# Two cached-attention decodes in one kernel: 4 MB loads of 32 KB descriptors, a softmax per four heads, and one TensorE loop

## The chip, the cores and the metric

The kernel runs on one core of a Trainium2 chip. The metric is the device time of one execution in microseconds (us). Four runs of the kernel before gave 249.22 to 249.61 us, with a median of 249.45 us. One further execution was profiled; its own time is 249.4 us, and all durations below come from it.

## The reference

Two independent attention decodes, A and B, of one token each. The model width is 576; there are 32 query heads, 16 key/value heads, a head size of 128, and a cache of 8192 positions. A looks only at the last 2048 positions, B at all 8192. The two results of 576 numbers stand side by side in the output. All tensors are bfloat16.

```python
def _A_ref(x, k_cache, v_cache, wq, wo):
    W = min(4096, max(256, Sk // 4))                       # 2048
    q = (x @ wq).reshape(B, Sq, Hq, Dh).transpose(0, 2, 1, 3)
    k = jnp.repeat(k_cache[:, :, Sk - W:, :], rep, axis=1)
    v = jnp.repeat(v_cache[:, :, Sk - W:, :], rep, axis=1)
    p = _softmax(jnp.einsum("bhqd,bhkd->bhqk", q, k) * (Dh ** -0.5), axis=-1)
    o = jnp.einsum("bhqk,bhkd->bhqd", p, v)
    return o.transpose(0, 2, 1, 3).reshape(B, Sq, Hq * Dh) @ wo
```

B is the same without the cut to W. Each input byte is used once: 8.4 MB each for A's K and V, 33.6 MB each for B's K and V, and 4.7 MB for each of the four weight matrices, 102.8 MB in all.

## The kernel before

**A planner.** The kernel is a list of operations, each with an engine, what it reads and what it writes (`Program.add`, L55). The planner derives semaphore waits from the list (`wants`, L104). Each engine runs its operations in the order in which they were added. SP issues all large loads, ACT issues the two loads of x. TensorE's (PE's) operations in the middle are folded into hardware loops (`looped`, L214 onwards): an outer loop over V rounds holds an inner loop over K rounds, and the waits of a loop body must be the same in every pass. All engines start after a barrier that the framework puts first (L743).

**Buffers.** `kslots` and `vslots` hold four slots each of 128 partitions x 16 KB (2 MB). `kt` holds four transposed units of 8 KB a partition. A load into a slot has to wait until the slot's last reader is done, and SP issues its loads strictly in order, so a load that waits holds back all that follow.

**Start.** wq of A goes into `vslots` 0 and 1 and a part of `kslots` 3, wq of B into `vslots` 2 and 3 and another part of `kslots` 3, each in loads of 2 MB, 2 MB and 0.5 MB (`load_wq`). x arrives as 128 rows of five bfloat16 numbers (`load_x`, L344); DVE masks it into `xpad` (L410), and PE multiplies it with wq (`q_part`, L425). `q_finish` turns the result into columns.

**K rounds.** There are five: round 0 is A's K, rounds 1 to 4 are B's. A round loads four slots. Each slot is two units; PE transposes a unit in 32 matmuls (L466), ACT and DVE evict them to `kt` (L472, L475), and PE multiplies the unit with the queries in 8 matmuls (L486) that add to the scores in `sacc`. B's round holds eight heads at 4096 positions, and two rounds share one `sacc`, one softmax and one run of 16 transposes of the weights (`softmax_exp`, `softmax_transpose` L536, `put` L545). `scores_zero` (L497) clears `sacc`. So there are three softmaxes.

**V rounds.** Five, each of four slots. Per slot PE runs 64 matmuls (`v_slot`, L557). DVE picks the diagonal blocks (`v_keep`, L566, and the sum of L373). The order on PE is K rounds 0 and 1, V 0, K 2 and 3, V 1, K 4, V 2, V 3, V 4.

**End.** Before V round 4 the last outer pass runs `weights` for A and B (L581 to L613: maximum, exponentials and sums over the parts, a chain of small steps through PE, DVE and ACT), and spreads A's output into `opj` (L630, L634). wo comes in nine loads: 14, 14 and 4 rows of A into `kslots` 0 to 2, 14 rows of B into `kslots` 3, and 8, 4, 3, 2 and 1 rows of B into `vslots` 0 and 1 (a row is 576 numbers a partition, 147,456 bytes over 128 partitions). All nine follow V round 4 on SP's queue. `wo_part` (L646) uses four matmuls a row; `finish_out` copies and stores.

Of the kernel before, what the change touches and what calls it, by code (L numbers as in the profile page):

```python
# [20 lines left out]
TS = 64  # L21
WQ_UNITS = 9
WQ_U = 2048
OUTW = DM // 4
# [14 lines left out]
class Program:  # L39
# [15 lines left out]
    def add(self, eng, fn, reads=(), writes=(), dma=None, after=(), tag=None, inc=1, loop=None):  # L55
        op = Op(eng, fn, tuple(reads), tuple(writes), dma, tag, 16 if dma is not None else inc, loop)
# [77 lines left out]
    def waits_of_loop(self, ops):  # L134
# [9 lines left out]
        for key, places in points.items():  # L144
# [26 lines left out]
            if len(fixed) == len(places):  # L171
                for place, hi in fixed.items():
# [4 lines left out]
                   for n in (1, 2, 16) for first in (0, n) if fits(first, n, some, taker)]  # L177
# [9 lines left out]
    def emit(self):  # L187
# [15 lines left out]
        def looped(eng, ops):  # L203
# [15 lines left out]
            def parts(of, i):  # L219
                todo = sorted(p for p in body if body[p].loop[3] == of)  # L220
                while todo:
                    cond = body[todo[0]].loop[2]
                    n = next((k for k, p in enumerate(todo) if body[p].loop[2] is not cond), len(todo))
                    if cond is None:
                        some(todo[:n])
                    else:
                        with eng.If(cond(i)):
                            some(todo[:n])
                    todo = todo[n:]

            with eng.Fori(0, self.outer) as v:
                with eng.Fori(*self.rounds_of(v)) as g:
                    parts("inner", g)
                parts("outer", v)

        def run(name, eng):
            ops = per[name]
            inside = [k for k, o in enumerate(ops) if o.loop]
            if not inside:
                plain(eng, ops)  # L240
                return
            lo, hi = inside[0], inside[-1] + 1
            assert len(inside) == hi - lo
            plain(eng, ops[:lo])
            looped(eng, ops[lo:hi])
            plain(eng, ops[hi:])

# [22 lines left out]
def bass_concat_heads__sliding_block_cached__gqa_block_cached__decode_kernel(  # L270
# [20 lines left out]


    G = [4, 2]
    CHUNK = [0, 1, 1, 2, 2]
    KIND = [0, 1, 2, 1, 2]
    base = [SK - W_A, 0]

    prog = Program(nc)
    add = prog.add
# [3 lines left out]
    kt = nc.alloc_sbuf_tensor("kt", [128, NKT, UNIT], BF16)  # L303
# [4 lines left out]
    pick = nc.alloc_sbuf_tensor("pick", [128, 4, 128], F32)  # L308
    same = nc.alloc_sbuf_tensor("same", [128, 128], F32)
    selq = nc.alloc_sbuf_tensor("selq", [128, 4], BF16)  # L310
    onesf = nc.alloc_sbuf_tensor("onesf", [128, 4], F32)
    zero = nc.alloc_sbuf_tensor("zero", [128, 512], BF16)
    qtm = nc.alloc_sbuf_tensor("qtm", [128, 3 * 256], BF16)
    qst = nc.alloc_sbuf_tensor("qst", [128, NS * 64], BF16)
    xtwo = nc.alloc_sbuf_tensor("xtwo", [128, 2, 8], BF16)
# [6 lines left out]
    srow = nc.alloc_sbuf_tensor("srow", [1, 2, 256], F32)  # L322
    diag = nc.alloc_sbuf_tensor("diag", [128, 2, DH, NS], F32)
    acc = nc.alloc_sbuf_tensor("acc", [128, 7, DH], F32)
# [11 lines left out]
    B_M = ("bank", 7)  # L336


    def load_x(P):
        def go(act):  # L340
            x = xs[P]
            with nc.allow_non_contiguous_dma(reason="small x load"):
                src = bass.AP(tensor=x.tensor, offset=x.offset, ap=[[9, 64], [4, 2], [1, 5]])
                return act.dma_start(xtwo[:, P, 0:5], src)  # L344
        add("act", go, writes=[("xtwo", P)], dma="x%d" % P)
# [5 lines left out]
    def setup(pool):  # L351
        for t in (ident, xpad, selq, zero, warm, qtm, identf, same, pick):
# [4 lines left out]
    add("pool", setup, writes=["ident", ("xpad", 0), ("xpad", 1), "selq", "ones", "warm", "zero", "identf", "pick", "same",  # L357
                               ("qtm", 0), ("qtm", 1), ("qtm", 2), ("opj", 0), ("opj", 1)])
# [13 lines left out]
    def sums(out, view, reads, writes, tag=None):  # L372
        add("dve", lambda dve: dve.tensor_reduce(out, view, AX.X, ALU.add), reads=reads, writes=writes, tag=tag)  # L373
# [5 lines left out]
    def load(dst, src, writes, dma, after=()):  # L379
        add("sp", lambda sp: sp.dma_start(dst, src()), writes=writes, dma=dma, after=after)  # L380

    def load_wq(P, k, dst, n, res):
        lo = 4 * k * WQ_U
        load(dst, lambda: wqs[P].rearrange("(m r) n -> m (r n)", m=64)
             .rearrange("m (e y) -> (m e) y", e=2)[:, lo:lo + n * WQ_U], [res], "wq%d%d" % (P, k))

    def load_kv(arrs, g, s, slots, name, after=()):
        P = 0 if g == 0 else 1
        i = s if g == 0 else 4 * ((g - 1) % 2) + s
        ch = 128 // G[P] * TS  # L390
        r0 = base[P] + (0 if g == 0 else (g - 1) // 2 * ch)

        def src():
            return arrs[P][0, i * G[P]:(i + 1) * G[P], r0:r0 + ch, :].rearrange("g (p t) d -> p g (t d)", t=TS)
        load(slots[:, s, :], src, [(name, s)], "%s%d" % (name, s), after)


    K_ON = lambda g: g < 5
    ODD = lambda g: (g & 1) == 1
    V_OF = {1: 0, 3: 1, 4: 2, 5: 3, 6: 4}  # L400

    def rounds_of(v):
        return v + 2 - (v < 2) - (v < 1), v + 3 - (v < 1)

    prog.rounds_of, prog.outer = rounds_of, len(V_OF)


    def x_columns(P):
        for e in range(2):
            add("dve", lambda dve, e=e: dve.tensor_scalar(xpad[:, P, 5 * e:5 * e + 5, 0], xtwo[:, P, 0:5],  # L410
                                                          par2[:, e:e + 1], None, ALU.mult),
                reads=[("xtwo", P), "par2"], writes=[("xpad", P)])
# [4 lines left out]
    def q_part(P, k, n, src, res):  # L417
        def mm(pe):
            for u in range(4 * k, 4 * k + n):
                for c in range(2):  # L420
                    for j in range(4):
                        n_ = 2 * j + c
                        x = u // 2 if n_ // 4 == u % 2 else 5 + (u + 1) // 2
                        o = (u - 4 * k) * WQ_U + (n_ % 4) * 512
# [3 lines left out]
        add("pe", mm, reads=[("xpad", P), res], writes=qbank)  # L428

    def q_finish(P):  # L430
# [13 lines left out]
        def put(dve):  # L444
            for e in range(2):
                if P == 0:
                    dst = bass.AP(tensor=qtm, offset=e, ap=[[768, 128], [4, 2], [34, 2], [72, 4]])
                else:
                    dst = bass.AP(tensor=qtm, offset=256 + e, ap=[[768, 128], [68, 2], [34, 2], [136, 4]])
                src = opsum[:, 0:32].rearrange("p (b a e j) -> p b a e j", b=2, a=2, e=2)[:, :, :, e, :]  # L450
                ins = dve.tensor_copy(dst, src)
            return ins
        add("dve", put, reads=[B_O], writes=[("qtm", 0)] if P == 0 else [("qtm", 1), ("qtm", 2)])

    def q_stage(g, s):
        o = KIND[g] * 256 + s * 64
        add("pool", lambda pool: pool.tensor_copy(qst[:, s * 64:(s + 1) * 64], qtm[:, o:o + 64]),  # L457
            reads=[("qtm", KIND[g])], writes=[("qst", s)], tag="q%d" % s)

    def k_transpose(g, u, place):  # L460
        s, half = divmod(u, 2)
        for q in range(4):
# [6 lines left out]
            add("pe", tr, reads=[("k", s), "ident"], writes=[("bank", q)], loop=(g, place + q / 8, K_ON, "inner"))  # L469
            dst = kt[:, u % NKT, q * 1024:(q + 1) * 1024]  # L470
# [8 lines left out]
    def k_scores(g, u, place):  # L479
        s, half = divmod(u, 2)  # L480

        def mm(pe):
            for e in range(2):
                for j in range(4):
                    rhs = kt[:, u % NKT, j * 1024:(j + 1) * 1024].rearrange("d (x g) -> d x g", g=2)[:, :, e]
                    ins = pe.matmul(sacc[32 * j:32 * j + 32, 512 * half:512 * half + 512],  # L486
                                    lhsT=qst[:, s * 64 + e * 32:s * 64 + e * 32 + 32],
                                    rhs=rhs, start=False, stop=True, skip_group_check=True)
            return ins
        add("pe", mm, reads=[("qst", s)] + [("kt", u % NKT, q) for q in range(4)], writes=[B_S[half]],  # L490
            loop=(g, place, K_ON, "inner"))

    def scores_zero(loop):
        for h in range(2):
            def mm(pe, h=h):
                for j in range(4):
                    ins = pe.matmul(sacc[32 * j:32 * j + 32, 512 * h:512 * h + 512], lhsT=zero[:, 0:32], rhs=zero[:, :],  # L497
                                    start=True, stop=True, skip_group_check=True)
                return ins
            add("pe", mm, reads=["zero"], writes=[B_S[h]], loop=loop and (loop[0], loop[1] + h / 8) + loop[2:])  # L500


    C_M, C_NB, C_L, C_W, C_AL, C_T = 0, 2, 4, 6, 8, 10
# [4 lines left out]
    def softmax_exp(c):  # L508
        P, k = (0, 0) if c == 0 else (1, c - 1)
# [18 lines left out]
    def softmax_transpose(g, place):  # L528
        for u in range(2):
# [9 lines left out]
            add("pe", tr, reads=["psb", "ident"], writes=[bank], loop=(g, place + u / 8, ODD, "inner"))  # L539
# [7 lines left out]
            add("dve", put, reads=[bank, "par2"], writes=[("ptm", u)], tag="put%d" % u, inc=1 if g == 1 else 2)  # L547


    def v_slot(vg, s, place, g):  # L550
# [10 lines left out]
        add("pe", mm, reads=[("ptm", 0), ("ptm", 1), ("v", s)], writes=[B_O], loop=(g, place, None, "outer"))  # L561

    def v_keep(g):
        def go(dve):
            m = bass.AP(tensor=rows, offset=KIND[g] * NS, ap=[[3 * NS, 128], [0, DH], [1, NS]])
            return dve.tensor_tensor(diag[:, g % 2, :, :], opsum[:, :].rearrange("p (s d) -> p d s", s=NS), m, ALU.mult)  # L566
        add("dve", go, reads=[B_O, "rows"], writes=[("diag", g % 2)])
        sums(acc[:, g, :], diag[:, g % 2, :, :], [("diag", g % 2), B_O], [("acc", g)], tag="ext")


    LAST = lambda v: v == 4

    def weights(P):
        n = 1 + P
        at = [(6, 18 + P + k / 8, LAST, "outer") for k in range(3)]
        m = C_M
        if n > 1:
            add("dve", lambda dve: dve.tensor_reduce(st(P, C_T), st(P, C_M, n), AX.X, ALU.max),
                reads=[("st", P, C_M + c) for c in range(n)], writes=[("st", P, C_T)])
            m = C_T  # L580
        add("pe", lambda pe: pe.matmul(misc[0:1, 0:128], lhsT=st(P, m), rhs=identf[:, :], start=True, stop=True),  # L581
            reads=[("st", P, m), "identf"], writes=[B_M], loop=at[0])
# [175 lines left out]
```

## Time and profile before

| what | value |
|---|---|
| median of four runs | 249.45 us |
| profiled execution, its own time | 249.4 us |
| its span, from the first to the last instruction | 248.0 us |
| PE busy | 169.9 us (69%) |
| ACT, DVE, POOL busy | 87.0, 81.0, 12.9 us |
| bytes read from HBM | 102.76 MB |
| SP waited for PE transposes (L466), in total | 85.0 us in 15 waits |
| SP waited for PE's V matmuls (L557), in total | 74.7 us in 14 waits |

The span is 1.4 us shorter than the execution's own time; that remainder lies outside the instructions. Busy time of an engine says how long its instructions ran, not whether anything waited for them. The 16 DMA engines of the core work beside the compute engines, and the page gives their busy share and the bytes they moved in 40 slices of 6.2 us. SP's waits are for buffers that are still in use; a wait delays the stream of bytes only where the DMA engines have nothing else left to move.

### The profile page before, as it was taken

Reading aid. Unit: us, or ns where it says so; the run is one execution under the profiler, and the core shown is the slowest. Engines: PE = TensorE matmul, PEld = TensorE weight load, DVE = VectorE, ACT = ScalarE, POOL = GpSimd, SP = SyncE. Lnnn points to the kernel's source line nnn. Section 1 sums busy time; section 2 is a strip of 40 time slices with the busy share of each in tenths; the row PEclk is TensorE's granted clock in tenths of the full one; section 3 lists DMA queues with packets and bytes.
Section 4 is the critical chain, followed back from the end, with each engine's and each line's share of the span. In section 5 each row is a group of like instructions: output and inputs, shape, how many; then the busy total and the mean of one; then the engine's idle time right before and its main releaser. Section 6 shows DMA issues by size and latency. Waiting matters only on the chain. (4 is left out here: it accounts for less than half of the span.)

```text
span 248.0 us, 7504 instructions
## 1 busy us (share of the span) xinstructions
PE 169.9 (69%) x3406; PEld 130.9 (53%) x3406; DVE 81.0 (33%) x152; ACT 87.0 (35%) x92; POOL 12.9 (5%) x49
## 2 busy tenths in 40 slices
PE   0174789984999569995999637998256144594634
PEld 0031267763777458864878427785244133484522
DVE  0010064663555026554555122656005004204000
ACT  2000066837378018876578004875300000000000
POOL 7500000000000000000000000000000000000000
PEclk9997599997799979999899965999858755557555
DMA  6999999999999999999999999999999999999993
GB/s 256 405 414 422 441 436 418 426 426 431 428 427 428 426 423 423 430 431 426 431 431 423 428 428 431 428 433 426 428 426 426 431 428 431 431 429 421 420 410 149
DMA packets 8236, 102.92 MB, mean 415 GB/s; under 512 B 1185, under 2 KB 1313, under 8 KB 2081
## 3 DMA queue, kind: packets, MB, share of 16 engines
q1 hardware_dynamic: 7936, 102.77, 98.0%
q8 instruction: 8, 0.13, 0.2%
q10 hardware_dynamic: 288, 0.00, 0.1%
q14 instruction: 4, 0.02, 0.0%
HBM read 102.76 MB, written 0.00 MB: 414 GB/s over the span
## 5 line engine op out<-in xcount | busy, mean ns | idle before, releaser
L472 ACT ACTIVATE kt<-ktps 128x1024 bf16<-128x1024 bf16 x80 | 77.7, 1021 | 52.1 <-PE ktps L466 52.1
L466 PEld LDWEIGHTS ktps<-ident,kslots 128*128 128x128 bf16 x1280 | 77.5, 102 | 26.1 <-issue 26.0
L466 PE MATMUL ktps<-ident,kslots 128*128 128x128 bf16 x1280 | 83.8, 228 | 10.5 <-PEq L214 10.4
L475 DVE COPY kt<-ktps 128x1024 bf16<-128x1024 bf16 x80 | 55.2, 691 | 51.3 <-PE ktps L466 51.3
L557 PE MATMUL opsum<-vslots,ptm 128*32 128x128 bf16 x1280 | 27.8, 260 | 28.4 <-PEq L214 24.4
L557 PEld LDWEIGHTS opsum<-vslots,ptm 128*32 128x32 bf16 x1280 | 24.9, 118 | 32.1 <-issue 32.0
L486 PE MATMUL sacc<-kt,qst 128*32 128x512 bf16 x320 | 25.9, 392 | 1.9 <-PEq L214 1.8
L566 DVE TENSOR_TENSOR diag<-opsum,rows 128x512 f32<-128x512 f32 x5 | 3.5, 692 | 56.0 <-PE opsum L557 56.0
L425 PE MATMUL opsum<-vslots,xpad 128*32 128x512 bf16 x64 | 8.6, 521 | 16.9 <-DVE xpad L410 11.3
L599 ACT ACTIVATE stat<-stat 128x1 f32<-128x1 f32 (+1 forms) x2 | 0.6, 294 | 37.3 <-DVE stat L597 37.3
L425 PEld LDWEIGHTS opsum<-vslots,xpad 128*32 128x32 bf16 x64 | 2.3, 122 | 20.3 <-issue 13.0
L457 POOL COPY qst<-qtm 128x64 bf16<-128x64 bf16 x20 | 4.5, 236 | 123.3 <-PE sacc L486 115.2
L431 ACT ACTIVATE qrow<-opsum 128x512 bf16<-128x512 f32 x2 | 1.2, 597 | 26.2 <-PE misc L425 26.2
L646 PE MATMUL ktps<-kslots,opj 128*32 128x144 bf16 x184 | 6.1, 326 | 5.8 <-DMA kslots<-in_B_wo_dram 3.9
L486 PEld LDWEIGHTS sacc<-kt,qst 128*32 128x32 bf16 x320 | 5.4, 95 | 8.8 <-issue 5.1
L523 ACT ACTIVATE psb<-sacc,stat 128x2048 bf16<-128x2048 f32 x3 | 5.9, 1967 | 8.5 <-DVE stat L517 8.5
L425 PE MATMUL misc<-vslots,xpad 128*32 128x512 bf16 x64 | 8.7, 523 | 0.0
L646 PEld LDWEIGHTS ktps<-kslots,opj 128*32 128x32 bf16 x184 | 5.2, 145 | 6.4 <-DMA kslots<-in_B_wo_dram 4.2
L433 DVE CAST qrow<-misc 128x512 bf16<-128x512 f32 x2 | 1.4, 692 | 17.8 <-PE misc L425 17.8
L630 PE MATMUL misc<-acc,pick 128*128 128x32 f32 x16 | 3.8, 404 | 3.6 <-DVE acc L624 2.9
L652 DVE CAST outsb<-ktps 128x144 bf16<-128x144 f32 x2 | 0.6, 308 | 16.1 <-PE ktps L646 16.1
L630 PEld LDWEIGHTS misc<-acc,pick 128*128 128x128 f32 x16 | 3.6, 328 | 3.8 <-DVE acc L624 3.0
(66 smaller groups left out, 63.0 us busy)
## 6 DMA issues: line engine op xcount, KB each, us to landing
kslots<-in_B_k_cache_dram SPq DMA_DIRECT2D x16, 2048.0 KB, 20.5
vslots<-in_B_v_cache_dram SPq DMA_DIRECT2D x16, 2048.0 KB, 18.8
kslots<-in_A_k_cache_dram SPq DMA_DIRECT2D x4, 2048.0 KB, 30.4
vslots<-in_A_v_cache_dram SPq DMA_DIRECT2D x4, 2048.0 KB, 25.1
vslots<-in_A_wq_dram SPq DMA_DIRECT2D x2, 2048.0 KB, 10.0
vslots<-in_B_wq_dram SPq DMA_DIRECT2D x2, 2048.0 KB, 20.5
kslots<-in_A_wo_dram SPq DMA_DIRECT2D x2, 2016.0 KB, 23.8
kslots<-in_B_wo_dram SPq DMA_DIRECT2D x1, 2016.0 KB, 31.2
```

What stands on the lines that cost most here:

```text
L425: ins = pe.matmul(qps[c][32 * j:32 * j + 32, :], lhsT=xpad[:, P, x, :], rhs=src[:, o:o + 512], start=(u == 0), stop=(u == WQ_UNITS - 1))
L433: add("dve", lambda dve: dve.tensor_copy(qrow[:, 512:1024], misc[:, :]), reads=[B_M], writes=[("qrow", 1)])
L457: add("pool", lambda pool: pool.tensor_copy(qst[:, s * 64:(s + 1) * 64], qtm[:, o:o + 64]), reads=[("qtm", KIND[g])], writes=[("qst", s)], ...
L466: ins = pe.matmul(ktps_bf[q][:, t * 128:(t + 1) * 128], lhsT=kslots[:, s, o:o + 128], rhs=ident[:, :], start=True, stop=True, is_transpose ...
L472: add("act", lambda act, q=q, dst=dst: act.activation(dst, ktps_bf[q], ACT.Copy), reads=[("bank", q)], writes=[("kt", u % NKT, q)], tag="e ...
L475: add("dve", lambda dve, q=q, dst=dst: dve.tensor_copy(dst, ktps_bf[q]), reads=[("bank", q)], writes=[("kt", u % NKT, q)], tag="e%d%d" % ( ...
L486: ins = pe.matmul(sacc[32 * j:32 * j + 32, 512 * half:512 * half + 512], lhsT=qst[:, s * 64 + e * 32:s * 64 + e * 32 + 32], rhs=rhs, start ...
L523: return act.activation(psb[:, :].rearrange("p (x g) -> p x g", g=2), src, ACT.Exp, bias=st(P, C_NB + k), scale=SCALE, accum_out=st(P, C_L ...
L557: ins = pe.matmul(opsum[32 * j:32 * j + 32, s * DH:(s + 1) * DH], lhsT=ptm[:, o:o + 32], rhs=vslots[:, s, b * 128:(b + 1) * 128], start=(u ...
L566: return dve.tensor_tensor(diag[:, g % 2, :, :], opsum[:, :].rearrange("p (s d) -> p d s", s=NS), m, ALU.mult)
L630: ins = pe.matmul(misc[:, 0:32], lhsT=pick[:, r, :], rhs=acc[:, d, 32 * r:32 * r + 32], start=(r == 0), stop=(r == 3))
L646: ins = pe.matmul(ktps[P][32 * j:32 * j + 32, 0:OUTW], lhsT=opj[:, P, jj:jj + 32], rhs=view[:, o:o + OUTW], start=(jj == 0), stop=(jj == H ...
```

## The change: what it does

1. **First load.** SP's first load is taken out of the block and put ahead of the drain of SP in the barrier that opens the program.
2. **x.** It is loaded as one row of 1152 bytes. DVE doubles its elements (`twice`), nine PE matmuls turn them into columns in `misc`, and DVE masks them into `xpad`.
3. **wq.** One load of 128 descriptors of 36 KB for each part: A's into `vslots` 0 to 2, B's into `kt`.
4. **B's K and V.** A load fills two neighbouring slots: 4 MB, two heads at all 8192 positions, 128 positions (32 KB) a partition. A's loads stay at 2 MB, two per pair. PE waits for both slots of a pair.
5. **Softmax.** A round of B now holds four heads with all positions, so each round has its own softmax: five in place of three. The first score matmul overwrites `sacc`, so `scores_zero` goes. B's four results need no sum over rounds; each is scaled and spread into its own 32 rows of `opj`.
6. **One PE loop of six rounds.** Each has K of round g (if g < 5) and V of round g-1 (if g > 0). A first part that runs in the last round only has the weights of A and B, the spreads of A and of B's first three rounds, and A's first 28 rows of wo.
7. **wo.** Seven loads. A's first 28 rows (32 KB descriptors) go into the first K pair and are issued before V round 4. A's last 4, and B's 17 (second K pair), 8, 4, 2 and 1 rows follow it.

The core of the diff:

```diff
+        first = per["sp"].pop(0)
+        one(self.nc.sync, first)
+        lead = self.nc.cur_bb.bb.instructions
+        ins = lead.pop()
+        at = next(k for k, o in enumerate(lead) if o.engine == ins.engine and "Drain" in str(o))
+        lead.insert(at, ins)
...
-                src = bass.AP(tensor=x.tensor, offset=x.offset, ap=[[9, 64], [4, 2], [1, 5]])
-                return act.dma_start(xtwo[:, P, 0:5], src)
+        add("act", lambda act: act.dma_start(xrow[0:1, P, :], xs[P][0]), writes=[("xrow", P)], dma="x%d" % P)
...
+    def load_pair(arrs, g, pi, slots, name):
+        key = "%s%d" % (name, pi)
+        if g == 0:
+            for s in (2 * pi, 2 * pi + 1):
+                load(slots[:, s, :], lambda s=s: arrs[0][0, s * 4:(s + 1) * 4, base:, :]
+                     .rearrange("g (p t) d -> p g (t d)", t=TS), [(name, s)], key)
+        else:
+            h0 = 4 * (g - 1) + 2 * pi
+            load(slots[:, 2 * pi:2 * pi + 2, :].rearrange("p s c -> p (s c)"),
+                 lambda: arrs[1][0, h0:h0 + 2, :, :].rearrange("g (p t) d -> p g (t d)", t=2 * TS),
+                 [(name, 2 * pi), (name, 2 * pi + 1)], key, inc=2)
...
-            add("pe", tr, reads=[("k", s), "ident"], writes=[("bank", q)], loop=(g, place + q / 8, K_ON, "inner"))
+            pair = [("k", s & ~1), ("k", s | 1)]
+            add("pe", tr, reads=pair + ["ident"], writes=[("bank", q)], loop=(g, place + q / 8, K_ON))
...
-                                    rhs=rhs, start=False, stop=True, skip_group_check=True)
+                                    rhs=rhs, start=(s == 0 and e == 0), stop=(s == NS - 1 and e == 1),
+                                    skip_group_check=True)
...
+    def spread(g, loop):
+        def mm(pe):
+            for r in range(4):
+                if g == 0:
+                    ins = pe.matmul(misc[:, 0:32], lhsT=pick[:, r, :], rhs=acc[:, 5, 32 * r:32 * r + 32],
+                                    start=(r == 0), stop=(r == 3))
+                else:
+                    c = g - 1
+                    ins = pe.matmul(misc[32 * c:32 * c + 32, 64:96], lhsT=pickb[:, r, :],
+                                    rhs=acc[:, 5 + g, 32 * r:32 * r + 32], start=(r == 0), stop=(r == 3),
+                                    skip_group_check=True)
...
+    order = [("k", 0, 0), ("k", 0, 1), ("v", 0, 0), ("k", 1, 0), ("k", 1, 1), ("v", 0, 1)]
+    order += [o for g in range(2, 5) for o in (("k", g, 0), ("k", g, 1), ("v", g - 1, 0), ("v", g - 1, 1))]
+    order += [("wo", 0), ("v", 4, 0), ("v", 4, 1)] + [("wo", i) for i in range(1, 7)]
...
+    for g in range(ROUNDS):
+        if g == 5:
+            weights(0)
+            weights(1)
+            scaled(0)
+            spread(0, (g, -7, LAST))
+            opj_put(0)
+            for c in range(1, 4):
+                scaled(c)
+                spread(c, (g, -7 + c / 8, LAST))
+            opj_put(1, 0, 96)
+            loads_until("wo", 0)
+            wo_part(0, *wo_loads[0][1:5], loop=(g, -6, LAST))
```

## The prediction

> **What bounds the kernel now.** I read the page's slices first, then the chain of waits, then the DMA queues cut into windows. The slices show DMA engines that never rest:
>
> ```profile
> DMA  6999999999999999999999999999999999999993
> GB/s 256 405 414 422 441 436 418 426 426 431 428 427 428 426 423 423 430 431 426 431 431 423 428 428 431 428 433 426 428 426 426 431 428 431 431 429 421 420 410 149
> ...
> q1 hardware_dynamic: 7936, 102.77, 98.0%
> ...
> q10 hardware_dynamic: 288, 0.00, 0.1%
> ```
>
> Columns of the queue rows are packets, MB and share of the 16 engines. PE is busy for 69%, and SP waits 160 us for buffers, yet no slice between the first and the last shows a gap: the waits are covered by loads already queued. The chain ends in the same way (start, duration, what):
>
> ```profile
> 221.39 23.81 DMA vslots<-in_B_wo_dram
> 245.20 0.04 issue
> 245.25 0.70 PE ktps L646 x12
> 245.97 0.31 DVE outsb L652
> ```
>
> So the time is: first byte, plus 102.8 MB at the rate of the stream, plus some 2.8 us from the last landing (245.2) to the end of the span (248.0), plus 1.4 us outside it (249.4 against 248.0). The sum below is made against 249.4 us, which is the median of the runs (249.45) but for 0.05. The bytes don't change. Three terms can: the start, the price of a packet, and the tail.
>
> **Packets (parts 3, 4, 7).** The 7936 packets are 55 loads of 128 data packets and 16 small ones, which is 7920, and 16 for the output: one descriptor is one packet, and an engine gets 9 packets of each load. After the change there are 2 loads for wq, 8 for A, 16 for B, 7 for wo: 33 loads, 22 fewer, so 198 fewer packets per engine. Their price must come from windows with different mixes (60 to 200 us, then 241 to 243 us):
>
> ```profile
> DMA packets 4107, 59.89 MB, mean 428 GB/s; under 512 B 451, under 2 KB 451, under 8 KB 451
> q1 hardware_dynamic: 4102, 59.82, 100.5%
> ```
>
> ```profile
> DMA packets 270, 0.82 MB, mean 408 GB/s; under 512 B 36, under 2 KB 55, under 8 KB 264
> q1 hardware_dynamic: 269, 0.80, 99.8%
> ```
>
> In the first each engine moved 3739 KB in 256.4 packets in 140 us, in the second 50 KB in 16.8 packets in 2.0 us. Two unknowns, time per KB and per packet, give 0.03675 us per KB (27.2 GB/s an engine) and 9.7 ns per packet. The window 240 to 243 (346 packets, 1.21 MB), less an instruction packet that took 2.2% of it, gives 6.2 ns in place of 9.7. I take 8 ns between them: 198 x 8 ns = 1.6 us saved. Upper end 2.1 us (10.5 ns, the last window without that deduction). The lower end is below zero: 32 KB descriptors aren't in the trace, and the slowest clean stretch of large descriptors, 16,128-byte ones of wo at 222 to 230 us, ran at 426 GB/s against 427.3 for the first window's own bytes; if B's 67.1 MB fell to that, 157.0 us would become 157.5, a loss of 0.5 us.
>
> Two rules of the Trainium skill stand against this term. In "DMA: Bandwidth & Descriptors", Specifications, the limit of HBM per core is about 358 GB/s and that of the fabric 435; the row of 428 GB/s refutes the first as a limit here, and by the second the whole stream could gain at most 102.77 MB x (1/427.5 - 1/435.2), an estimate of 4.3 us. The same page, under Latency and other measured facts, has HBM copies slow down when the pitch between partitions is a large power of two, with 512 KiB its smallest case; the change doubles B's pitch from 16 to 32 KB, which it doesn't cover. By it the sum stays as it is.
>
> **The x load (part 2).** x now takes 256 of 10 bytes and 32 small packets. While they run, until 16 us, the stream is slower; the last two columns are DMA share and GB/s:
>
> ```profile
> 4.00:12.00 8.00, 0.69 (x8) 0.35 (x12) 0.65 (x3) 0.00 (x0) 5.07 (x14) 1.00 0.99 410
> 12.00:16.00 4.00, 4.00 (x56) 1.86 (x52) 0.00 (x0) 0.00 (x0) 0.00 (x0) 1.00 0.99 398
> 16.00:60.00 44.00, 31.76 (x469) 20.99 (x462) 17.57 (x33) 20.09 (x22) 1.71 (x8) 0.87 1.01 427
> ```
>
> Lost against 427: 8 x 17/427 + 4 x 29/427 = 0.59 us. Some of that belongs to the 128 small wq descriptors counted above. I take 0.4 us, between 0 and 0.59. The new PE and DVE work on x (two doublings of 1152 elements on one partition, 18 tiny matmuls, four masks) sits ahead of `q_part`. Priced by the 1024-element reductions of 1.23 us and 164 ns per small matmul of `q_finish`, it is 2 x 1.4 + 18 x 0.16 + 4 x 0.23 = 6.6 us; it is hidden by the wq load, which lands only at about 12 us. Even uncovered it would delay queries that K needs at 33 us.
>
> **The first load (part 1).** SP's first DMA starts at 0.74 us, behind a barrier wait of 0.7 us, and its first bytes move at 1.7. Ahead of the drain it can start up to 0.74 us earlier; less the fetch of the instruction, I take 0.55. The other end: if the drain waits until that load has landed, the second load is issued at 12 us and the stream has a hole of the 0.96 us between issue and first byte, so a loss of 1.0 us. No row shows a drain with a load ahead of it; I take the nearest, the issue of a 2 MB load, which holds SP for 0.43 us only.
>
> **Whole pairs, fewer and later releases (parts 4, 6).** A load of 4 MB needs two free slots, and SP's queue stands behind it. With the first byte at 1.2 us and 9.8 us per 4.2 MB, landings are: wq 23, K0 33 and 43, V0 first pair 53, K1 62.5 and 72, V0 second pair 82, then K2's first pair until 92. K2's first load must be issued by 82 and needs K1's first pair transposed: 62.5 + 4.47 (two units after a pause, 64 matmuls) + 2.8 (softmax transposes and their puts, 62.98 to 65.82) + 2 x 2.46 (a unit with its scores) = 74.7. The margin is 7 us, and later rounds have the same or more: per round PE needs some 20 + 2.8 + 4 to 7.4 us for V, in 39.2 us of stream. The two extra softmaxes (max 1.23, exponential 1.97, 16 transposes) lie in the 39.2 - 30 us that PE and ACT have free each round; without that cover they'd cost 2 x 6 us. `scores_zero` goes, 2.8 us of PE that nothing waited for. All this: 0.
>
> **The tail (parts 5 to 7).** Call L the landing of V round 4's last pair. Before, nine wo loads (9.4 MB, 22 us) followed it; now 36 rows do, 5.31 MB, 12.4 us. So compute behind V 4 has less cover. Work between V 3's landing and L, which lie 12.5 MB or 29.3 us apart, from the rows of before: 2 slots at 1.90, a pause of 1.3, the weights 8.4 (207.10 to 215.52), A's spread 1.9, hand-over on DVE 0.7, three B spreads of 0.8 to 1.92 (a quarter of the weight columns, same passes), 112 matmuls of wo at 2 x 1.87, softmax transposes 2.8, 2 slots 3.8: 28.8 to 32.2 us. After L: 2 slots 3.8, diagonal and sum 1.4, scaling 0.3, spread 0.8 to 1.9, copy 0.3, 68 matmuls 2.3, then 60 more 2.0, in all 10.9 to 12.0. So the last matmul can run 10.9 to 14.9 us after L, the last bytes land at 12.4. Lateness 0 to 2.5 us; PE's V slots after dense work took 1.08 in place of 1.90 (223.51), which takes 1.6 off, so I take 0.05. The last loads stay small (8, 4, 2, 1 rows), so the 2.8 us after landing stay.
>
> **Sum.** 249.4 - 1.6 - 0.4 - 0.55 + 0.05 = 246.9 us.
>
> **Rivals.**
>
> *The stream has one rate.* Packet price is an artefact of the small loads' ends, and 32 KB buys nothing. For it: 230 to 236 us, with 4.6 KB descriptors in it, still ran at 426. Against it: the two windows above. Only start and x count: 249.4 - 0.95 = 248.4 us.
>
> *The tail decides.* PE is at the low clock (granted 0.50 from 230 us on), the B spreads cost 1.9 each, and the last matmuls come 1.5 us behind the bytes: 246.9 + 1.5 = 248.4 us. Against it: the shorter weight load.
>
> *Slower: PE falls behind the pairs.* Place: SP's wait ahead of K2's or K3's first pair. At the low clock a unit takes 3.57 + 0.66 = 4.2 us, a round 8 x 4.2 + 2.8 + 7.6 = 44 us against 39.2: 4.8 us lost per round, which the 7 us margin covers once. It decides from the second such round on; with three slow rounds 14.4 - 7 = 7.4 us, less the gains: 254 us. For it: after each pause PE starts slow (59.62, 3.57 us for 32 transposes). Against it: before, the clock rose within one unit, and units were 2.46 apart.
>
> **How the numbers follow.** Forecast 0.62, with 246.0 to 247.9 as its own range (packet price 1.2 to 2.1 and start 0.3 to 0.74 on the good side, x at 0 and a tail of 0.6 on the other). One rate 0.17, tail 0.09, PE behind 0.12. What a measurement of this kernel tells from no change is about 0.2%, 0.5 us. Faster: all of the forecast, nearly all of the two at 248.4: 0.86. Same 0.04, slower 0.10 (part of the last lands near zero). The range goes from 245.9 to 249.0, which leaves out the last rival and little else.
>
> **What would show it.** Right: the first load's issue near 0.1 us; mean rate in the middle 430 to 431 GB/s; 4.1 to 12 us near 420 or more; the last wo landing about 2.5 us earlier, at 242.7, followed by under 1 us of matmuls. Wrong: 427 in the middle (one rate); a last matmul group whose idle before it isn't a DMA (tail); a slice with DMA share below 9 in the middle (PE behind); a hole at 12 us (drain).

## The result: no difference in the ratio, and runs that scatter

| | before | after |
|---|---|---|
| median of all runs | 249.55 us (54 runs) | 250.12 us (34 runs) |
| lowest and highest | 248.99, 249.96 us | 247.70, 253.98 us |
| profiled execution, its span | 249.4, 248.0 us | 248.96, 247.5 us |

The ratio is 1.0002, with a 95% interval from 0.999 to 1.0014. It is formed without the nine runs of the changed kernel that lie over 1.5% above its fastest, so the median over all runs, 0.57 us later than before, is the less flattering figure. The forecast was 246.9 us, its range 245.9 to 249.0: the result lies outside. More telling than the median is the spread: 6.3 us where the kernel before had 1.0.

The page of the changed kernel, slices and queues:

```profile
DMA  9999999999999999999999999999999999999992
GB/s 352 411 453 397 422 426 437 424 461 424 336 426 412 447 437 416 426 425 455 424 429 434 434 424 434 429 429 434 445 429 429 429 435 428 429 429 430 416 405 76
...
q1 hardware_dynamic: 4768, 102.76, 97.6%
q8 instruction: 10, 0.16, 0.3%
```

The packets are exactly the forecast's count (7936 less 22 x 144 is 4768). The busy share shows no gap, and read alone it would clear the stream. The row of GB/s doesn't: the eleventh slice, 62 to 68 us, moves 336. Cut into windows (PE, PEld, DVE, ACT and POOL busy, granted clock, DMA share, GB/s):

```profile
16.00:60.00 44.00, 30.55 (x437) 20.94 (x430) 13.23 (x33) 15.52 (x17) 1.47 (x7) 0.88 1.00 425
60.00:80.00 20.00, 13.09 (x195) 10.82 (x196) 10.35 (x16) 10.68 (x12) 0.47 (x2) 0.83 0.99 401
80.00:200.00 120.00, 93.44 (x2081) 76.80 (x2080) 53.79 (x83) 62.76 (x64) 2.60 (x11) 0.89 1.01 432
```

From 80 us on the stream has the higher rate, 432 GB/s against 428 before. Between 60 and 80 us it loses 20 x 31/432 = 1.4 us, at a DMA share of 0.99: packets that wait for their data count as busy. The kernel before ran at 429 there:

```profile
60.00:80.00 20.00, 20.00 (x291) 16.16 (x289) 10.50 (x17) 13.04 (x14) 0.71 (x3) 0.86 1.01 429
```

The chain of the changed kernel still ends on the last loads of wo:

```profile
210.05 34.72 DMA kt<-in_B_wo_dram
244.77 0.04 issue
244.82 0.69 PE ktps L655 x12
245.51 0.02 issue
245.53 0.31 DVE outsb L661
```

The landing that the chain names, of the load before the last, comes 0.43 us earlier than before (244.77 against 245.20), and 2.75 us of span follow it, 2.76 before.

**Where the stream is late.** The timeline of the changed kernel, PE's transposes and SP's issues in K rounds 0 and 1 (start, duration, what; in brackets the idle time ahead of it and its releaser; PEq is PE's sequencer):

```profile
35.43 1.44 PE L478 MATMUL ktps<-ident,kslots 128*128 128x128 bf16 x12 [3.81 <-PEq L216]
38.14 4.69 PE L478 MATMUL ktps<-ident,kslots 128*128 128x128 bf16 x52 [1.27 <-issue]
...
47.91 1.63 PE L478 MATMUL ktps<-ident,kslots 128*128 128x128 bf16 x26 [1.62 <-issue]
...
49.56 11.84 SPq L388 DMA_DIRECT2D kslots<-in_B_k_cache_dram  x2
...
56.72 1.62 PE L478 MATMUL ktps<-ident,kslots 128*128 128x128 bf16 x25 [1.21 <-issue]
...
61.44 1.24 SPq L388 DMA_DIRECT2D vslots<-in_A_v_cache_dram  x2
...
68.91 5.33 PE L478 MATMUL ktps<-ident,kslots 128*128 128x128 bf16 x64 [6.54 <-PEq L216]
```

The same place in the kernel before:

```profile
32.54 3.78 PE L466 MATMUL ktps<-ident,kslots 128*128 128x128 bf16 x64
...
36.35 16.39 SPq L380 DMA_DIRECT2D kslots<-in_B_k_cache_dram  x4
```

Before, B's first K load left at 36.35 us, when one slot was transposed. Now PE starts 2.9 us later, as it waits for the pair; after that it stands still three times (1.27, 1.62 and 1.21 us) for no reason that the profile names ("issue"); and the load leaves at 49.56, when the whole pair is done. The issue of the next pair, 60.83 us, is the end of the two-load group at 49.56 less its own 0.57.

From the trace's packet records I took, for each load, the mean over the 16 engines of when its last packet ended. The "lead" is that time of the load ahead minus the issue of this one; "late" is the distance between the two ends beyond what the packets' sizes need (8.5 ns and 1 us per 27.2 KB). "After, repeated" is a second profile of the changed kernel, shown below:

```
after            issue   lead  late      after, repeated  issue   lead   late
K1 first pair    49.56   3.83  0.10                       51.38   1.95   0.68
K1 second pair   60.83   2.38  1.30                       63.75   0.00   2.21
K2 first pair    80.07   3.95  0.07                       85.17   0.35   1.84
K2 second pair   89.90   3.91  0.31                       94.99   2.08   0.71
K3 first pair   111.30  11.98 -0.01                      115.39  11.57  -0.03
```

So a load needs some 4 us of lead to lose next to nothing. With next to no lead the stream loses about 2.2 us less the lead (0.00 and 0.35 us here). In between the mean lead doesn't fix the loss: at 1.95 to 2.38 us it was 0.68 to 1.30. Only K rounds 1 and 2 are thin. What stands ahead of the prediction, that SP's wait delays the stream only when the DMA engines have nothing else left to move, is therefore too weak a condition: the load has to leave some microseconds before that.

### The profile page after: what moved, and what is told of

Same layout as the page of the kernel before. It is cut to its first block, busy times and chain, and to the rows that moved or that the text cites. A ratio compares the mean times of both kernels' runs of the same rounds, so it can differ in the third digit from the quotient of the medians.

```text
span 247.5 us, 7533 instructions
## 1 busy us (share of the span) xinstructions
PE 165.4 (67%) x3446; PEld 131.7 (53%) x3446; DVE 90.0 (36%) x169; ACT 91.6 (37%) x96; POOL 13.0 (5%) x49
## 3 DMA queue, kind: packets, MB, share of 16 engines
q1 hardware_dynamic: 4768, 102.76, 97.6%
## 5 line engine op out<-in xcount | busy, mean ns | idle before, releaser
L478 PE MATMUL ktps<-ident,kslots 128*128 128x128 bf16 x1280 | 87.0, 232 | 28.7 <-PEq L216 24.6
L478 PEld LDWEIGHTS ktps<-ident,kslots 128*128 128x128 bf16 x1280 | 80.6, 105 | 43.6 <-issue 43.6
L563 PE MATMUL opsum<-vslots,ptm 128*32 128x128 bf16 x1280 | 25.4, 252 | 21.7 <-PEq L216 17.7
L563 PEld LDWEIGHTS opsum<-vslots,ptm 128*32 128x32 bf16 x1280 | 23.8, 114 | 23.8 <-issue 23.8
L529 ACT ACTIVATE psb<-sacc,stat 128x2048 bf16<-128x2048 f32 x5 | 9.8, 1967 | 13.4 <-DVE stat L523 13.4
L415 PE MATMUL misc<-ident,xdup 1*128 1x1 bf16 x18 | 0.8, 162 | 11.2 <-DVE xdup L409 11.2
L521 DVE TENSOR_REDUCE stat<-sacc 128x1 f32<-128x1024 f32 x5 | 6.1, 1225 | 3.6 <-PE sacc L500 3.5
L435 PE MATMUL opsum<-kt,xpad 128*32 128x512 bf16 x36 | 4.5, 490 | 3.8 <-DMA kt<-in_B_wq_dram 3.8
L435 PE MATMUL opsum<-vslots,xpad 128*32 128x512 bf16 x36 | 4.7, 512 | 1.9 <-DMA vslots<-in_A_wq_dram 1.9
L551 DVE TENSOR_SCALAR ptm<-misc,par 128x512 bf16<-128x512 bf16 x10 | 4.3, 477 | 4.3 <-PE misc L542 4.3
```

Of the source, the lines that this page charges most:

```text
L435: ins = pe.matmul(qps[c][32 * j:32 * j + 32, :], lhsT=xpad[:, P, x, :], rhs=src[:, o:o + 512], start=(u == 0), stop=(u == WQ_UNITS - 1))
L478: ins = pe.matmul(ktps_bf[q][:, t * 128:(t + 1) * 128], lhsT=kslots[:, s, o:o + 128], rhs=ident[:, :], start=True, stop=True, is_transpose ...
L521: add("dve", lambda dve: dve.tensor_reduce(st(P, C_M + k), sacc[:, :], AX.X, ALU.max), reads=B_S, writes=[("st", P, C_M + k)], tag="max")
L529: return act.activation(psb[:, :].rearrange("p (x g) -> p x g", g=2), src, ACT.Exp, bias=st(P, C_NB + k), scale=SCALE, accum_out=st(P, C_L ...
L551: ins = dve.tensor_scalar(to, src, par2[:, e:e + 1], None, ALU.mult)
L563: ins = pe.matmul(opsum[32 * j:32 * j + 32, s * DH:(s + 1) * DH], lhsT=ptm[:, o:o + 32], rhs=vslots[:, s, b * 128:(b + 1) * 128], start=(u ...
```

## The experiments

Times are medians, with lowest, highest and number of runs; ratios are to the kernel before on the same chips (249.5 to 249.6 us).

**The first load alone.** The kernel before, with only the first load moved ahead of the barrier's drain:

```diff
+        first = per["sp"].pop(0)
...
+        one(self.nc.sync, first)
+        lead = self.nc.cur_bb.bb.instructions
...
+        lead.insert(at, ins)
```

> The kernel before with the first load alone moved ahead of SP's drain. Prediction's step: 0.55 us less, at most 0.74, so 248.9 us for 249.5. Rival (the drain or the barrier waits): 249.5 or more, and the second load is issued late. In the changed kernel's trace the first load starts at 0.00 and the second at 0.81, so the hole isn't expected.

248.83 us (248.58 to 249.25, 9), ratio 0.9974 (0.9963 to 0.9984): 0.7 us, nearly the 0.74 by which the issue moved. The timeline of the changed kernel shows that nothing stands behind the drain:

```profile
0.00 0.39 SPq L388 DMA_DIRECT2D vslots<-in_A_wq_dram  x1
...
0.81 0.33 SPq L388 DMA_DIRECT2D kt<-in_B_wq_dram  x1
```

**Release of one place earlier.** A's second V pair is split and half of it put ahead of K1's second pair, so that this pair has 4.9 us more bytes ahead of it:

```diff
-    order = [("k", 0, 0), ("k", 0, 1), ("v", 0, 0), ("k", 1, 0), ("k", 1, 1), ("v", 0, 1)]
+    order = [("k", 0, 0), ("k", 0, 1), ("v", 0, 0), ("k", 1, 0), ("v", 0, 1, 0), ("k", 1, 1), ("v", 0, 1, 1)]
```

> The changed kernel with one thing moved: A's second V pair is two loads of 2 MB, and the first of them is issued ahead of the second pair of K round 1, where SP waits for PE. Late release (theory): in the changed kernel that K load is issued at 60.8 us while its forerunner's bytes end at 62.9 to 65.0 us, and the landings there lie 10.7 to 11.0 us apart instead of 9.7. With 4.9 us of other bytes in between, the gap goes: landings 9.7 apart plus 4.9 for the half, packets of 32 KB near 1.215 us throughout, median 247 to 248 us, and the runs lie within 1 us. Rival A (the spread of 247.7 to 254 comes with 32 KB descriptors themselves): median near 250, spread as wide as before. Rival B (instruction packets of 16 KB that hit one DMA engine twice): the median falls by no more than 0.5 us, the last landing still trails the first engine by 3 us.

249.9 us (248.18 to 253.12, 13), ratio 0.9995 (0.9978 to 1.0012). No measurable gain, and a miss: 247 to 248 us was expected. In its profile, taken of the latest of these runs, the second pair of K1 has 4.95 us of lead and is late by 0.11 only, but K1's first pair (0.65 us, late 1.72) and K2's first (-0.27 us, late 2.41) are now the thin ones. So one place isn't the whole cause; the runs below ask whether PE's lateness in all of the first rounds is.

**16 KB descriptors, pair waits kept.** As the last one, and B's K and V in loads of 2 MB, while waits and releases stay those of pairs:

```diff
+            for e in range(2):
+                load(slots[:, 2 * pi + e, :],
+                     lambda e=e: arrs[1][0, h0:h0 + 2, :, :].rearrange("g (p e t) d -> e p g (t d)", e=2, t=TS)[e],
+                     [(name, 2 * pi + e)], key)
```

> The kernel of e1_half_v with B's K and V pairs as two loads of 2 MB with 16 KB descriptors on the same semaphore; waits stay those of a pair. Price of a packet (prediction: 8 ns, 9 packets per load and engine): 16 loads more are 144 packets per engine, 1.2 us more than e1_half_v. Rival (one rate whatever the descriptor): the same time as e1_half_v within 0.3 us. If 32 KB descriptors make the runs vary, this one is narrow while e1_half_v is wide; by late release both are narrow.

250.81 us (249.23 to 252.2, 11), ratio 1.004 (1.0018 to 1.0061): 0.9 us more than the last one, where 1.2 were expected. Descriptors of 32 KB aren't needed for a late stream or for a spread of 3 us: with leads of 2.20, 1.59 and 2.32 us the loads are late by 0.62, 0.69 and 1.35 here too.

**A wait and a release per slot.** The changed kernel with all K and V in 2 MB loads, each with its own semaphore; PE waits for one slot:

```diff
...
-            pair = [("k", s & ~1), ("k", s | 1)]
+            pair = [("k", s)]
...
```

> The changed kernel with all of K and V in loads of 2 MB with 16 KB descriptors, each slot with its own semaphore, waited for and released by itself as in the kernel before. Late release: K round 0 starts at its first slot (near 30.5 to 32 us for 35.4), each load waits for one slot only, the stream has no stretch with packets beyond 0.7 us, and the runs are as narrow as before's (1 us). The packet price takes 1.2 to 1.4 us: 247.0 (e4_less_pe's 247.7 less the 0.7 us that its landings still lost) + 1.3 = 248.3 us. Rival (packets and the start are all that counts, pairs don't matter): 249.9 + 1.3 = 251 us, wide.

248.92 us (248.81 to 249.3, 11), ratio 0.9974 (0.9966 to 0.9983): narrow, and 0.6 us above the 248.3 expected. Against the last experiment, whose loads have the same size, 1.9 us less (1.6 by the ratios), and the spread falls from 3.0 to 0.5 us. The two differ in the wait and release of a pair, and in the half V load put ahead, which alone changed nothing measurable (249.9 us). That points to the pair's wait and release; which of the two counts more isn't separated.

**Less work on PE.** The changed kernel without the eighth unit of each K round, its transposes, evictions and score matmuls (so its scores are incomplete):

```diff
...
-                k_transpose(g, u, 5 + 2 * u)
+                if u < 7:
+                    k_transpose(g, u, 5 + 2 * u)
...
-            k_scores(g, 7, 21)
```

> The changed kernel with the eighth unit of each K round left out of PE, ACT and DVE (its 32 transposes, evictions and 8 score matmuls; all loads stay). The second K pair is released 2.5 us earlier in each round. Late release: K round 1's second load is issued near 58.4 us in place of 60.8, the gap of 1.0 to 1.3 us shrinks to under 0.3, median 247 to 248 us with fewer high runs. Rivals A and B: no change, median near 250 with the same spread, since the loads, descriptors and instructions fetched are all but the same.

247.88 us (247.38 to 248.31, 6), ratio 0.993 (0.9916 to 0.9943). All bytes still move, so the 2.2 us against the changed kernel's median were lateness of PE and of the engines that evict for it, which reached the stream though PE is busy for 67% of the span.

**The first part of the loop moved.** The part that runs in the last round only stands in the code ahead of K; here it is put between K and V:

```diff
-                spread(c, (g, -7 + c / 8, LAST))
...
-            wo_part(0, *wo_loads[0][1:5], loop=(g, -6, LAST))
...
+                spread(c, (g, 26 + c / 8, LAST))
...
+            wo_part(0, *wo_loads[0][1:5], loop=(g, 27, LAST))
```

> The changed kernel with the part for the last round moved from ahead of the K part to between K and V; the same instructions, the same loads. Code fetch (theory): the 20 KB of instructions that the first five rounds jump over lie between the start and K's code, PE sits 1.2 to 3.4 us three times in K round 0 while a 16 KB instruction packet lands, and 4 us at the start of K round 1. With K's code right behind what runs before it, K round 0 is done 2 us or more earlier, the loads of K rounds 1 and 2 are issued earlier, median 248 to 249. Rival (PE is late because it waits for pairs; fetches cost the same wherever the part stands): median 249.5 to 250, as wide as the changed kernel.

251.5 us (250.29 to 253.26, 6), ratio 1.0089 (1.0057 to 1.0121): the opposite of what I expected. Its timeline:

```profile
46.94 10.63 SPq L388 DMA_DIRECT2D kslots<-in_B_k_cache_dram  x2
...
72.75 5.03 PE L478 MATMUL ktps<-ident,kslots 128*128 128x128 bf16 x64 [14.21 <-PEq L216]
```

K round 0 has no standstill any more and the first load that waits for its slots leaves 2.6 us earlier. But PE now stands for 14.2 us ahead of K round 1, the last 7.9 of them after its first pair had landed (64.88 us), and K2's first pair leaves at 83.62 with a lead of -0.54 us: late by 2.59. The standstills moved with the code.

**A's K by slot.** PE starts K round 0 on one slot. B's loads stay at 4 MB; the first slot counts on the load, and SP signals the second when it issues the load:

```diff
...
+                 after=[(name, 2 * pi + 1)] if k_ else ())
...
-            pair = [("k", s & ~1), ("k", s | 1)]
+            pair = [("k", s)]
```

> The changed kernel; A's four K loads count on a semaphore of their own each, so PE starts K round 0 at the first 2 MB instead of the first pair; B's 4 MB loads stay, their second half is signalled by SP at issue. Late release: K round 0 runs 4.9 us earlier, K round 1's loads are issued near 45 and 56 us (49.6 and 60.8 in the changed kernel) and no longer run dry; K round 2's first load, which depends on round 1, may still lose up to 1 us. Median 247.5 to 248.5, spread at most 2 us. Rival (fetch stalls alone): no change beyond 0.5 us.

250.36 us (248.01 to 254.55, 12), ratio 1.0021 (0.9995 to 1.0047). A miss: PE starts at 32.16, runs 12 matmuls, and then stands for 4.40 us at the same matmul as in the changed kernel. Data weren't what it lacked.

**Both.** The last two together:

> e6_last_behind_k and e7_k0_by_slot together. If both causes of lateness are real, all K loads are issued 3 us or more before the bytes ahead of them end, and what is left is the prediction's sum: 246.9 us, runs within 1 us. If only one is real, the better of the two. If neither, 250.

248.31 us (246.68 to 249.39, 12), ratio 0.995 (0.9933 to 0.9967): better than either alone, but short of the 246.9 us and the spread of 1 us that were expected. K1's pairs have leads of 12 us, K2's 3.1 us, and the loads of K2 are late by 0.05 and 0.64.

**What PE stands for.** In these places the page's "instruction" queue q8 moves a packet of 16,384 bytes: code. The changed kernel's DMA queues in 45 to 47 us, where PE's second standstill begins:

```profile
q1 hardware_dynamic: 55, 0.88, 105.2%
q8 instruction: 1, 0.02, 3.2%
```

From the packet records (start and end of the code packet) and the timelines (PE goes on); the repeated run and "K alone by slot" follow below:

```
                  code packet     PE goes on   after its end
after             35.60-36.65     38.14        1.49
                  45.48-46.50     47.91        1.41
                  54.17-55.19     56.72        1.53
  round 1         65.35-66.43     68.91        2.48
after, repeated   37.37-38.43     39.71        1.28
                  47.20-48.22     49.73        1.51
                  57.29-58.17     59.64        1.47
  round 1         69.61-70.55     73.06        2.51
A's K by slot     35.03-36.08     37.40        1.32
                  44.88-45.90     47.41        1.51
K alone by slot   37.23-38.29     39.70        1.41
                  46.85-47.88     49.28        1.40
  round 1         66.65-67.73     70.25        2.52
```

PE goes on 1.3 to 1.5 us after the packet's end inside round 0, and 2.5 us after it at the start of round 1, wherever the packet falls. There are nine such packets up to 102 us and none from there until 242 us: the loop's first rounds fetch its code, later ones don't. Not every such packet stops PE: in the kernel before two of them (from 39.51 and 47.16 us) fall into K round 0, and with the first part moved two more (44.36, 51.94), and PE has no standstill there. The kernel before has one of 3.96 us in its first V round, which ends 1.49 us after a packet (86.39 to 87.40). The record doesn't name the engine that fetches; that these are PE's is inferred from the fixed distance. The Trainium skill, "Runtime: NRT & Kernel Launch", section "Instruction fetch mechanics", has code fetched in blocks of 16 KiB by the sequencer's own DMA queue, with the cost of a block mostly hidden and a stall after a taken branch. The size agrees; the blocks of the table are not hidden, and there the measured standstills decide.

**The changed kernel again.** Once more with a profile, to tie the spread to the standstills:

> The changed kernel again, beside the others on one chip. Late release: median near 250 and runs over 4 us; the profile, whichever run it catches, has K loads issued less than 4 us before the bytes ahead of them end, and the landings behind each such load come late by about 2.4 us less that lead, down to zero. Rival (the variation lies outside the loads): late landings don't add up to the difference between this run and 247.5 us.

250.57 us (247.92 to 253.01, 12), ratio 0.9992 (0.9964 to 1.002); the profiled run took 252.63 us, its span 251.1. Its timeline:

```profile
39.71 5.21 PE L478 MATMUL ktps<-ident,kslots 128*128 128x128 bf16 x52 [2.70 <-issue]
...
51.38 12.93 SPq L388 DMA_DIRECT2D kslots<-in_B_k_cache_dram  x2
...
59.64 1.62 PE L478 MATMUL ktps<-ident,kslots 128*128 128x128 bf16 x25 [2.31 <-issue]
...
64.36 1.24 SPq L388 DMA_DIRECT2D vslots<-in_A_v_cache_dram  x2
...
73.06 6.25 PE L478 MATMUL ktps<-ident,kslots 128*128 128x128 bf16 x64 [7.79 <-PEq L216]
```

Same program, standstills of 2.70 and 2.31 us in place of 1.27 and 1.21, and the four K loads of the table above are late by 5.4 us in place of 1.8. The difference, 3.6 us, is that of the spans (251.1 against 247.5). The granted clock is 0.84 in both, so it isn't PE's clock.

**K alone by slot.** B's K comes in 2 MB loads, and every slot of K, A's too, has its own wait and release; V and wq keep the large descriptors, and V its pairs:

```diff
...
+            if name == "k":
+                for e in range(2):
+                    load(slots[:, 2 * pi + e, :],
+                         lambda e=e: arrs[1][0, h0:h0 + 2, :, :].rearrange("g (p e t) d -> e p g (t d)", e=2, t=TS)[e],
+                         [(name, 2 * pi + e)], "k%d" % (2 * pi + e))
+                return
...
-            pair = [("k", s & ~1), ("k", s | 1)]
+            pair = [("k", s)]
```

> The changed kernel with B's K (alone) in 2 MB loads of 16 KB descriptors, a semaphore, a wait and a release for each slot; V stays in 4 MB pairs of 32 KB descriptors. Late release of K's pairs (theory): the issue of V's loads was never late in any run (9 us or more ahead), so giving up pairs on K alone is enough to make the runs as narrow as e5_slotwise (0.5 us), and V's larger descriptors give back 8 loads x 9 packets x 8.6 ns = 0.6 us: 248.3 us. Rival (4 MB loads or 32 KB descriptors of any tensor make the time vary): a spread of 2 us or more.

248.27 us (248.21 to 248.47, 5), ratio 0.9945 (0.9932 to 0.9959): better than both kernels. Timeline and the window of 60 to 80 us:

```profile
39.70 5.06 PE L484 MATMUL ktps<-ident,kslots 128*128 128x128 bf16 x52 [5.66 <-issue]
...
44.79 17.82 SPq L388 DMA_DIRECT2D kslots<-in_B_k_cache_dram  x4
```

```profile
60.00:80.00 20.00, 12.99 (x182) 10.74 (x179) 9.88 (x16) 10.11 (x11) 0.47 (x2) 0.83 1.01 426
```

PE's standstill is the longest seen in K round 0, 5.66 us, and the stream doesn't feel it: every K load has 6 us of lead or more, and the window runs at 426 in place of 401. The spread is 0.26 us over its five runs.

**The same with the first part moved.** The last experiment, and the loop's first part between K and V:

> e9_k_by_slot with the last round's part between K and V, as in e6_last_behind_k. Where PE's lateness no longer reaches SP, it doesn't matter where the part stands: 248.3 us, the same as e9_k_by_slot within 0.4 us, although the same move cost the changed kernel 1.4 us. Rival (code fetch itself costs time, by its packets on the DMA engines or PE's stalls): 1 us or more above e9_k_by_slot.

248.25 us (247.68 to 248.63, 5), ratio 0.9949 (0.9935 to 0.9962). Where the code stands no longer matters.

**x as before.** K alone by slot, and x in its 10-byte pieces:

```diff
...
+                src = bass.AP(tensor=x.tensor, offset=x.offset, ap=[[9, 64], [4, 2], [1, 5]])
+                return act.dma_start(xtwo[:, P, 0:5], src)
```

> e9_k_by_slot with x loaded as before, 128 rows of five numbers straight to DVE, no doubling and no PE columns. Prediction's step: the small packets cost 0.4 us (0 to 0.59), so 248.65 us for 248.27; 4 to 16 us runs near 410 GB/s in place of 436. Rival (the small packets cost nothing, the slow start of before was the 2 MB loads of wq): 248.3 us within 0.15.

248.9 us (248.65 to 249.41, 11), ratio 0.998 (0.9971 to 0.9989): x is worth 0.6 us by the medians, 0.2 by the two profiled spans. But the stretch that the forecast ascribed to it isn't slow here:

```profile
4.00:12.00 8.00, 0.00 (x0) 0.00 (x0) 0.29 (x1) 0.06 (x1) 5.21 (x14) 1.00 1.02 438
12.00:16.00 4.00, 0.00 (x0) 0.00 (x0) 0.00 (x0) 0.00 (x0) 0.00 (x0) 1.00 1.01 433
```

Before, these windows ran at 410 and 398 GB/s; with K alone by slot and the new x, at 443 and 442. What slowed them there beside the smaller packets of wq isn't settled.

## Why the prediction failed, step by step

The table sets the terms against three profiles, in us against the profile of before. All ends are those of the semaphores. Packets are worked out from the price measured below. "x, start" is by how much earlier the last load of wq ends on the mean of the engines (25.81 us before), beyond the first load and the packets of wq's four loads fewer. "Late K loads" is the sum of "late" over the K loads of rounds 1 and 2, less the 0.31 that the same bytes showed before.

| term | forecast | after | after, repeated | K alone by slot |
|---|---|---|---|---|
| first load | -0.55 | -0.74 | -0.74 | -0.74 |
| packets | -1.6 | -1.68 | -1.68 | -1.07 |
| x, start of the stream | -0.4 | -0.59 | -0.63 | -0.61 |
| late K loads | 0 | +1.40 | +5.08 | +0.16 |
| rest | | +0.05 | +0.11 | +0.13 |
| mean end of the stream | -2.55 | -1.57 | +2.14 | -2.14 |
| last engine behind the mean | 0 | +1.13 | +1.01 | +1.21 |
| from last landing to the end | +0.05 | 0.00 | 0.00 | -0.01 |
| span | -2.5 | -0.44 | +3.15 | -0.95 |

**The failed step is "Whole pairs, fewer and later releases", and in it "The margin is 7 us ... All this: 0".** That zero measured +1.4 us in one profile and +5.1 in the other. Its working priced K2's first pair with PE starting when data land and never standing still, and counted the margin up to the landing of the load ahead, so with no lead at all, where some 4 us are needed. K2's first pair left at 80.07, not 74.7: K1's first pair landed 2.5 us later than forecast (65.0 against 62.5), and PE, ahead of which a code packet stood, began 3.9 us after that, at 68.91. The softmax transposes took 1.0 us where 2.8 were put, or it would have been later still. And it named no margin for K1's two pairs: by its own rows the second would have left at 52 (43 + 4.47 + 2 x 2.46); it left at 60.83, after a start 2.4 us late and 4.1 us of standstills in K round 0, and with 2.4 us of lead it was late by 1.3, most of the loss in that run. In the repeated run all four pairs were late. That the pairs are the cause is shown by the runs with one wait and release per slot, where longer standstills cost nothing, beside the run with 16 KB descriptors and pair waits, which stayed late. That the ratio came out at 1.000 is chance: some 3 us of gains met a lateness that varies from run to run.

**Unforeseen: the last engine.** The end isn't set by the mean of the 16 DMA engines but by the slowest. In the last load of wo it lands 1.01 us behind the mean before, 2.14 after. So of the 1.57 us by which the stream ends earlier, 0.44 arrive. (The 245.2 us that the prediction takes for the last landing is that of the load before the last; the last came at 245.56.) In the changed kernel the distance between first and last engine jumps from 2.3 to 3.5 us over K2's second pair, beside the code packet at 102.13. Whether code packets cause it isn't shown: with the first part moved there are two fewer (8 against 10), and the lag is 2.07 all the same, or 1.56 with K by slot as well.

**Right: the price of a packet.** Packet durations, by size, in the records: 51 ns at 1152 bytes, 178 at 4608, 612 at 16 KB, 1214 at 32 KB, 1364 at 36 KB. That is 8.5 ns and 27.2 GB/s an engine, where the forecast took 8 ns. All slotwise against only K slotwise differ by 8 loads of 9 packets, 0.61 us by this price; 0.65 was measured between the medians, on two chips. The rival of one rate is out: 432 GB/s, with 435 the fabric's ceiling in the Trainium skill, "DMA: Bandwidth & Descriptors", Specifications.

**Right: first load and tail.** The tail of the changed kernel waits for DMA alone:

```profile
239.90 2.23 PE L655 MATMUL ktps<-kslots,opj 128*32 128x144 bf16 x68 [1.06 <-DMA kslots<-in_B_wo_dram]
...
242.71 1.15 PE L655 MATMUL ktps<-kt,opj 128*32 128x144 bf16 x32 [0.58 <-DMA kt<-in_B_wo_dram]
244.08 1.40 PE L655 MATMUL ktps<-kt,opj 128*32 128x144 bf16 x28 [0.21 <-DMA kt<-in_B_wo_dram]
```

**x: size about right, reason not.** 0.2 to 0.6 us against 0.4, but not in the windows that the forecast derived it from: with the old x they run near 435 GB/s. In the run with the old x the table's row is -0.36, so 0.25 us of it are x and the rest the way wq is loaded.

**The rivals.** "PE falls behind the pairs" had the place nearly right (SP's wait ahead of K2's first pair) and the mechanism wrong: not a low clock round after round (0.83 to 0.89 granted) but the first rounds alone, through code and pairs. Its size, 254 us, is that of the latest run only. The sign to watch was wrong too: a DMA share below 9 never came; the GB/s row showed it.

## What to carry to other kernels

Joining two buffers into one load halves the packets, but it also makes the release wait for the last reader of both, and a strict queue passes that on; price the lead of every such load in the first rounds, not one in the steady state, and want some 4 us. Take the large descriptors where the reader is early (here V, wq, wo) and keep the small unit where the reader is late (K): in that form the change took 1.3 us off the kernel. A spread that grows with an edit is a finding by itself: profile a late run as well.

## What the runs showed of the hardware

- A load whose predecessor's bytes end less than some 4 us after its issue leaves the stream partly dry (late by 0.07 to 0.31 us at leads of 3.8 to 4, by 2.2 at none), while its packets count as busy: 32 KB packets took up to 2.73 us in place of 1.21.
- The first rounds of a large loop body fetch code in 16 KB packets (about 1 us each) through the same DMA engines. Where the part for the last round stood ahead of K, PE stood for 1.1 to 5.7 us beside most such packets in K round 0; in the kernel before, and with that part moved, it didn't stand there. How late the packet starts varies from run to run, and why isn't recorded.
- The slowest of the 16 DMA engines ended 0.8 to 2.9 us behind their mean, and the program ends with it.
